# The first expert item of a fused attention and two expert layers: layer 1 in the attention's banks, half of its weights unsplit, two of its loads issued after the rows' gather

## The chip, the cores and the metric

One core of a Trainium2 chip runs the whole program. The metric is the device time of one execution in microseconds, the median of several runs. Every time below is in microseconds from the start of the program's span unless it is called a duration.

## The reference

Three layers in a row, all in f32: block-causal attention over 2 batches, 8 heads, 576 positions and 64 columns; an expert layer that sends each of the 1152 rows to the one of 8 experts with the largest logit; a second expert layer of the same size with a capacity of 288 rows per expert.

```python
scores = scale * np.matmul(q, k.transpose(0, 1, 3, 2))      # blocks of 64, masked above the diagonal
attn = np.exp(scores - np.max(scores, axis=-1, keepdims=True))
attn = attn / (np.sum(attn, axis=-1, keepdims=True) + 1e-09)
x = np.matmul(attn, v)                                      # then (1152, 512)

e_idx = np.argmax(x @ w_gate, axis=1)                       # per row one expert e
h = np.maximum(x[mask] @ w1[e], 0.0)                        # (rows, 512) x (512, 1024)
ye = h @ w2[e]                                              # (rows, 1024) x (1024, 512)
out[mask] = gate_w[mask, None] * eom[mask, e, None] * ye
```

The second layer has no output gate `eom` and leaves out the rows of an expert beyond its capacity.

## The kernel before

**Products.** TensorE multiplies f32 matrices exactly enough only in four passes, or as three one-pass products of `float32r` operands. The kernel splits each weight chunk (128 x 1024) into a high part, `wh = round(raw)`, which is a cast on ScalarE (`split_hi`, L147), and a low part, `wl = raw - wh`, a subtraction on VectorE (`split_lo`, L165). The rows are split the same way (`xh`, `xl` in `xprep`, L607 and L608; `hh`, `hl` between the layers). A product is then `xh*wh + xh*wl + xl*wh`: three products of 128 x 512 (L618 for layer 1, L632 for layer 2).

**Items.** An expert's rows are worked in items of 128 rows. Each item needs 8 chunks of weights, 4 of `w1` (512 x 1024) and 4 of `w2` (1024 x 512, two 128-row halves per chunk), in the tile `raw` (8 x 128 x 1024 f32, 512 KB a chunk), and its 128 rows, which an indirect DMA of POOL gathers from the attention's output in DRAM (`gather_rows`, L182). Layer 1 multiplies 4 row chunks by 4 weight chunks for each of two halves of 512 columns, relu on ScalarE (L677) brings a half to `hs`, four transposes (L713) turn it, `hh` and `hl` split it (L714, L716), and layer 2 adds 8 steps of three products into one bank. An item whose expert is that of the item before skips its loads.

**The order.** The attention part is put in order by a scheduler of the framework. From `tc.manual_schedule()` on, each engine runs its instructions in the order in which the code writes them. The first item (item 0) is prepared while the last head's attention runs: `begin_first` picks the expert of the first three blocks of rows (`route_first`), loads the four `w1` chunks once the expert is known (`first1["e"]`), gathers the rows once their numbers are known (`first1["ig"]`), and then loads the four `w2` chunks (`first1["e2"]` is the same expert's number, computed again after the rows' numbers, so that these loads are issued after the gather). Chunks 0 to 2 of `w1` are split beside the last attention products, and the cast of chunk 3 follows the last of the copies `ot` of the attention output (L1127 to L1129).

**Passing over.** The last steps of a head are: four f32 products with 64 columns of weights each (L1124), three copies to `ot` on ScalarE, two products with a matrix that sorts rows and adds the gate logits (L1138 and L1139), then on VectorE the scaling of the rows (L1142) and of the logits (L1144) and their sum (L1146). After it the attention's PSUM pools (`ps_s`, two tiles of two banks; `ps_t`, four banks) are closed and the expert layers' pool `ps_m` takes all eight banks (`PH` 2, `PX` 4, `PY` 1, `PR` 1). Only then does `xprep` transpose the gathered rows (L605).

**Route and first item.** `Moe.begin` weaves item 0 with the routing of all other rows: `step1` finds each row's expert (its last operation writes the one-hot `ohx`, L204), `step2` ranks rows on TensorE (L438, L440), `step3` is a chain of small VectorE operations (from `rko`, L448, to the last `ohp`, L497), `step4` gets every item's row numbers from 18 small products (L520) and writes them (`ig`, L522). Gathers of items 1 and 2 and the loads of item 1 follow. `go(n)` issues the first `n` products of layer 1; `parts(i)` transposes half `i`.

```python
some(split_hi, his, 2)
R.step1()
splits()
some(split_hi, his, 2)
go(n)
R.step2()
...
go(n1 // 2 + 3)
low0 = parts(0)
go(n1)
```

Here `his` are the casts of the four `w2` chunks, `splits` is `xl` and the low part of `w1` chunk 3. After layer 2 comes `xprep` of item 1 (L605, L607, L608), and item 1 goes on in `second` and `layers`.

Of the kernel before, what the change touches and what calls it, by code (L numbers as in the profile page):

```python
# [7 lines left out]
F32 = mybir.dt.float32  # L8
# [23 lines left out]
def kernel(  # L32
# [569 lines left out]
    def xprep(xg, ps, later=False):  # L602
# [5 lines left out]
        low = lambda: V.tensor_tensor(xl, ps, xh.bitcast(F32), op=ALU.subtract)  # L608
        if later:
            return (xh, xl), low  # L610
        low()
        return xh, xl

    def l1_steps(out_, xs, w, c, cols):
        xh, xl = xs
        wh, wl = w
        for j, (l, r) in enumerate(((xh, wh), (xh, wl), (xl, wh))):
            yield nc.tensor.matmul(out_, l[:, c * P : (c + 1) * P], r[:, cols], start=(c == 0 and j == 0), stop=(c == KD - 1 and j == 2))  # L618
# [5 lines left out]
    def l2_mm(y, ts, ws, f, start=None, stop=None):  # L624
        th, tl = ts[f // 4]
        wh, wl = ws[f // 2]
# [3 lines left out]
        rs = slice((f % 2) * 512, (f % 2 + 1) * 512)  # L630
        for j, (l, r) in enumerate(((th, wh), (tl, wh), (th, wl))):
            nc.tensor.matmul(y, l[:, cs], r[:, rs], start=(first and j == 0), stop=(last and j == 2))  # L632
# [11 lines left out]
    class Moe:  # L644
# [22 lines left out]
        def first_layer1(self, xs, ws):  # L667

            hs = HS.next()
            for i in range(2):  # L670
                ps = PH.next()
                n = 0
                for c in range(KD):
                    for _ in l1_steps(ps, xs, ws[c], c, slice(i * 512, (i + 1) * 512)):
                        n += 1
                        if n == 3 * KD:
# [3 lines left out]
        def begin(self, l1, n, gone, w2_done, splits):  # L680


            R, st = self.R, self.st
            n1 = 6 * KD
# [8 lines left out]
            his, los = iter(range(KD + w2_done, 2 * KD)), iter(range(KD + w2_done + (self.m == 2), 2 * KD))  # L693
# [15 lines left out]
            def parts(i):  # L709
                ps, th, tl = PX.next(), HH.next(), HL.next()  # L710
                h = self.h[:, i * 512 : (i + 1) * 512]
                for c in range(4):
                    nc.tensor.transpose(ps[:, c * P : (c + 1) * P], h[:, c * P : (c + 1) * P], ident)  # L713
                nc.scalar.copy(th, ps)  # L714
                ht.append((th, tl))
# [13 lines left out]
            for _ in range(2 if self.m == 1 else 0):  # L729
# [709 lines left out]
```

## Time and profile before

| | |
|---|---|
| median of three runs (lowest, highest) | 453.9 us (451.9, 454.22) |
| the profiled execution: its own time, its span | 451.8 us, 450.0 us |
| busy, share of the span: TensorE, VectorE, ScalarE, POOL | 92%, 82%, 73%, 22% |
| the chain that ended last: TensorE, VectorE, ScalarE, nothing seen | 70%, 15%, 6%, 6% |
| mean granted TensorE clock | 0.988 |
| q1 (loads and stores), q0 (gathers and scatters) | 54.62 MB, 10.63 MB |

The profile is of one execution, and all durations below are of that one. The span runs from the first to the last instruction; the execution's own time is 1.8 us more. Shares of busy time are means over stages with different limits: attention up to about 135 us, the first expert layer to about 307, then the second. A chain of waits goes back from the last instruction, at each step to whatever released it; the row of a step tells when it began and how long it ran on the chain. In the timeline the note in brackets is the time the engine stood idle before an instruction and what ended it. PE is TensorE, PEld its weight load, DVE VectorE, ACT ScalarE, SP the engine that issues the loads.

### The profile page before, as it was taken

The numbers are of one execution on the slowest core, as the hardware profiler recorded it, in microseconds if no ns is written. First come the engines' busy times: TensorE is split into PE (matmuls) and PEld (weight loads), VectorE is DVE, ScalarE is ACT, GpSimd is POOL, SyncE is SP. The second block draws the span as 40 slices with busy tenths as digits, with TensorE's granted clock in tenths as the row PEclk, the third lists the DMA queues.
The fourth block names the chain that finished last, engine by engine and source line by source line (L and its number), as shares of the span: only waits on it lengthen the run. The fifth ranks groups of instructions, "written<-read, shape, count | busy, mean of one in ns | idle before, by whom it ended". The sixth has DMA issues, their size and how long they took to land.

```text
span 450.0 us, 8362 instructions
## 1 busy us (share of the span) xinstructions
PE 414.7 (92%) x2501; PEld 334.0 (74%) x2501; DVE 368.4 (82%) x816; ACT 327.9 (73%) x617; POOL 99.0 (22%) x182
## 2 busy tenths in 40 slices
PE   3899999999988998999997999978989999999993
PEld 2677888877766776788876888755768888888872
DVE  8666776766799999989899796778899999999930
ACT  3678787787775889577868474645959988888930
POOL 8501221121020312033202203102303611111100
PEclk9999999999998999999999899999999999999998
DMA  5567532311074210199519102914628418995000
GB/s 133 110 175 243 133 79 53 82 28 52 20 280 153 72 47 18 32 320 338 194 47 360 63 13 83 348 49 133 259 95 311 146 52 305 395 375 206 24 31 8
DMA packets 58245, 65.99 MB, mean 147 GB/s; under 512 B 34080, under 2 KB 38688, under 8 KB 58180
## 3 DMA queue, kind: packets, MB, share of 16 engines
q1 hardware_dynamic: 54660, 54.62, 37.0%
q0 software_dynamic: 3520, 10.63, 6.8%
q8 instruction: 25, 0.41, 0.4%
q14 instruction: 40, 0.33, 0.2%
HBM read 109.66 MB, written 11.01 MB: 268 GB/s over the span
## 4 chain that ended last, share of the span: by engine, by line
PE 70%; DVE 15%; ACT 6%; issue 6%; DMA 1%; POOLq 0%; POOL 0%; DVEq 0%; ACTq 0%
PE ph L618 21%; PE py L632 20%; PE s L1071 7%; PE pst L1124 6%; PE pst L1098 5%; DVE wl L165 4%; PE px L1311 3%; PE px L605 2%; ACT p L1075 2%; DVE wl_a L165 2%; PE pst L1051 2%; PE px L1358 1%; DVE i128b L99 1%; DVE wl_b L165 1%; PE s L1068 1%
## 5 line engine op out<-in xcount | busy, mean ns | idle before, releaser
L165 DVE TENSOR_TENSOR wl<-raw,wh 128x1024 fp32r<-128x1024 f32 x84 | 98.8, 1217 | 2.6 <-ACT wh L147 2.5
L147 ACT CAST wh<-raw 128x1024 fp32r<-128x1024 f32 x84 | 82.7, 1058 | 1.0 <-DMA raw<-in_moe_w_dram 0.9
L618 PE MATMUL ph<-wh,xh 128*128 128x512 f32 x168 | 69.8, 416 | 2.5 <-ACT xh L607 2.1
L618 PE MATMUL ph<-wl,xh 128*128 128x512 f32 x168 | 67.0, 399 | 1.0 <-DVE wl L165 1.0
L618 PE MATMUL ph<-wh,xl 128*128 128x512 f32 x168 | 67.2, 400 | 0.1
L165 DVE TENSOR_TENSOR wl_a<-raw,wh_a 128x1024 fp32r<-128x1024 f32 x44 | 52.0, 1216 | 0.8 <-ACT wh_a L147 0.3
L147 ACT CAST wh_a<-raw 128x1024 fp32r<-128x1024 f32 x44 | 43.9, 1068 | 7.0 <-DMA raw<-in_moe_w_dram 7.0
L1072 DVE TENSOR_REDUCE mx<-s 128x1 f32<-128x256 f32 (+8 forms) x72 | 34.4, 486 | 17.7 <-PE s L1071 6.2
L165 DVE TENSOR_TENSOR wl_b<-raw,wh_b 128x1024 fp32r<-128x1024 f32 x40 | 47.4, 1219 | 0.9 <-ACT wh_b L147 0.5
L1075 ACT ACTIVATE p<-s,mx 128x256 f32<-128x256 f32 (+8 forms) x72 | 37.8, 527 | 10.0 <-DVE mx L1072 9.0
L147 ACT CAST wh_b<-raw 128x1024 fp32r<-128x1024 f32 x40 | 39.3, 1065 | 0.0
L1098 PE MATMUL pst<-ident,p 128*128 128x128 f32 x200 | 38.6, 286 | 0.4 <-DVE lg L1144 0.3
L618 PEld LDWEIGHTS ph<-wl,xh 128*128 128x128 f32 x168 | 32.1, 191 | 9.2 <-DVE wl L165 3.4
L618 PEld LDWEIGHTS ph<-wh,xh 128*128 128x128 f32 x168 | 31.9, 190 | 8.9 <-ACT xh L607 2.8
L618 PEld LDWEIGHTS ph<-wh,xl 128*128 128x128 f32 x168 | 31.9, 190 | 8.3 <-DVE xl L608 1.7
L632 PE MATMUL py<-wh_a,hh 128*128 128x512 f32 x88 | 35.9, 408 | 0.4 <-ACT hh L1319 0.4
L632 PE MATMUL py<-wh_a,hl 128*128 128x512 f32 x88 | 35.2, 400 | 0.8 <-DVE hl L716 0.5
L632 PE MATMUL py<-wl_a,hh 128*128 128x512 f32 x88 | 35.0, 398 | 0.0
L1302 ACT ACTIVATE hs<-ph 128x512 f32<-128x512 f32 x38 | 22.3, 602 | 16.9 <-PE ph L618 15.5
L641 POOL DMA_INDIRECT x2d<-ys,io x8 | 11.9, 1483 | 95.3 <-ACT ys L640 87.1
L1320 DVE TENSOR_TENSOR hl<-px,hh 128x512 fp32r<-128x512 f32 x38 | 24.4, 681 | 9.9 <-ACT hh L1319 9.9
L632 PE MATMUL py<-wh_b,hh 128*128 128x512 f32 x80 | 32.3, 404 | 0.0
(298 smaller groups left out, 901.5 us busy)
## 6 DMA issues: line engine op xcount, KB each, us to landing
raw<-in_moe_w_dram SPq DMA_DIRECT2D x184, 512.0 KB
out_dram<-zrow SPq DMA_DIRECT2D x9, 256.0 KB
kn<-in_k_dram SPq DMA_DIRECT2D x16, 128.0 KB
qn<-in_q_dram SPq DMA_DIRECT2D x16, 128.0 KB
vn<-in_v_dram SPq DMA_DIRECT2D x16, 128.0 KB
x1d<-x SPq DMA_DIRECT2D x3, 576.0 KB
x2d<-zrow SPq DMA_DIRECT2D x3, 256.0 KB
x1d<-x SPq DMA_DIRECT2D x3, 192.0 KB
```

What stands on the lines that cost most here:

```text
L147: nc.scalar.copy(whs[i], raw[:, c, :])
L165: V.tensor_tensor(wls[i], raw[:, c, :], whs[i].bitcast(F32), op=ALU.subtract)
L618: yield nc.tensor.matmul(out_, l[:, c * P : (c + 1) * P], r[:, cols], start=(c == 0 and j == 0), stop=(c == KD - 1 and j == 2))
L632: nc.tensor.matmul(y, l[:, cs], r[:, rs], start=(first and j == 0), stop=(last and j == 2))
L1071: nc.tensor.matmul(ps[:, a:z], s[l][:, b, :], s[r][:, a - o : z - o], start=(j == 0), stop=(j == 2))
L1072: V.tensor_reduce(out=s["mx"][:, t : t + 1], in_=ps[:, o : o + n], op=ALU.max, axis=AX.X, negate=True)
L1075: nc.scalar.activation(s["p"][b][:, 0:n], ps[:, o : o + n], AF.Exp, bias=s["mx"][:, t : t + 1], accum_out=s["sm"][:, t : t + 1])
L1098: last[0] = nc.tensor.transpose(ps[:, j * P : (j + 1) * P], s["p"][b][:, c * P : (c + 1) * P], ident).ins
L1124: nc.tensor.matmul(po[r, 0 : n * BLK], nat["v"][h % NR["v"]][:, c, r], w[:, :, r], start=(c == 0), stop=(c == nc_ - 1))
L1302: nc.scalar.activation(hs[:, i * 512 : (i + 1) * 512], hp[i], AF.Relu)
L1311: nc.tensor.transpose(ps[:, c * P : (c + 1) * P], hs[:, o : o + P], ident)
L1320: V.tensor_tensor(tl, tps[i], th.bitcast(F32), op=ALU.subtract)
```

## The change

For item 0 of the first layer alone:

- **Banks.** The attention pools stay open longer (`banks`, closed by `open_banks` inside `begin`, after the routing's `step3` is issued). The gathered rows are transposed into an attention bank `pst`, on TensorE's queue ahead of the last four attention products, and layer 1's two halves go to a tile `hp0` of `ps_s`.
- **Whole chunks.** Chunks 2 and 3 of `w1` and chunks 0 and 1 of `w2` are not split: one f32 product of `raw` with unsplit rows stands for three. The rows are first copied unsplit, `xn` (in `YS.t[1]`), and only their first 256 columns are split, from `xn`; `hn` is the unsplit first half of the turned `hs`. The whole products come first in each half.
- **Loads.** Chunks 0 and 1 of `w1` are loaded as before; chunks 2 and 3 are loaded after the gather, ahead of the `w2` chunks.
- **Order in `begin`.** The two casts that are left for `w2` are issued after `parts(0)`, the second half's transposes come after `step3`, one of layer 2's steps ahead of `step4` and three behind it.
- **Last head.** The logits are scaled before the rows (L1144 and L1142 change places for the last head).

```diff
-    def l1_steps(out_, xs, w, c, cols):
-        xh, xl = xs
-        wh, wl = w
-        for j, (l, r) in enumerate(((xh, wh), (xh, wl), (xl, wh))):
-            yield nc.tensor.matmul(out_, l[:, c * P : (c + 1) * P], r[:, cols], ...)
+    def l1_steps(out_, xs, w, c, cols, start=None, stop=None):
...
+        if w is None:
+            yield nc.tensor.matmul(out_, xs[2][:, cs], raw[:, c, cols], start=start, stop=stop)
+            return
+        for j, (l, r) in enumerate(((xs[0], w[0]), (xs[0], w[1]), (xs[1], w[0]))):
+            yield nc.tensor.matmul(out_, l[:, cs], r[:, cols], start=start and j == 0, stop=stop and j == 2)
...
     def l2_mm(y, ts, ws, f, start=None, stop=None):
...
+        if ws[f // 2] is None:
+            nc.tensor.matmul(y, th[:, cs], raw[:, KD + f // 2, rs], start=first, stop=last)
+            return
...
+            order = sorted(range(KD), key=lambda c: ws[c] is not None)
+            self.half = sum(3 if w else 1 for w in ws)
...
-            some(split_hi, his, 2)
+            if m == 2:
+                some(split_hi, his, 2)
             R.step1()
             splits()
-            some(split_hi, his, 2)
+            if m == 2:
+                some(split_hi, his, 2)
             go(n)
             R.step2()
...
+                if ws2[2 * i] is None:
+                    ht.append((HN, None))
+                    nc.scalar.copy(HN, ps)
+                    return lambda: None
...
-            go(n1 // 2 + 3)
+            go(self.half + 3)
             low0 = parts(0)
-            go(n1)
+            if m == 1:
+                some(split_hi, his, 2)
+            go(2 * self.half)
             chain, regs, places = R.step3(), R.registers(), R.places_a()
...
+            if m == 1:
+                open_banks()
+                low1 = parts(1)
+                self.y = PY.next()
+                l2(0, 1)
             some(split_lo, los, 1)
             low0()
             R.step4()
...
             some(split_lo, los, 4)
+            if m == 1:
+                l2(1, 4)
...
-                    load_w(w11, w12, first1["e"], 0, KD)
+                    load_w(w11, w12, first1["e"], 0, 2)
                 yield
             xg = item0["xg"] = XG.next()
             g = gather_rows(xg, x1d[0 : NA * P, :], first1["ig"]).ins
-            load_w(w11, w12, first1["e2"], KD, 8)
+            load_w(w11, w12, first1["e2"], 2, 8)
...
-        for c, (w, h, pk) in ((1, ("ot", H - 1, 1)), (2, ("tp", H - 1, 2)), (3, ("ot", H - 1, 2))):
-            with tc.issue_after(anchors[w, h, pk]):
-                item0["w1"].append(split(c) if c < KD - 1 else split_hi(c))
+        with tc.issue_after(anchors["ot", H - 1, 1]):
+            item0["w1"] += [split(1), None, None]
         ctx.enter_context(tc.manual_schedule())
+
+        ps, xn, xh, xl = pst(), YS.t[1], XH.next(), XL.next()
+        for c in range(KD):
+            nc.tensor.transpose(ps[:, c * P : (c + 1) * P], item0["xg"][:, c * P : (c + 1) * P], ident)
+        z = 2 * P
+        with tc.issue_after(anchors["ot", H - 1, 2]):
+            nc.scalar.copy(xn, ps)
+            nc.scalar.copy(xh[:, 0:z], xn[:, 0:z])
...
-    one.begin(one.first_layer1(item0["xs"], item0["w1"]), 2, 0, 0, first_splits)
+    hp0 = ps_s.tile([P, 1024], F32, tag="s", name="hp0")
+    one.begin(one.first_layer1(item0["xs"], item0["w1"], [hp0[:, 0:512], hp0[:, 512:1024]]), 4, 0, 0, 2, first_low)
```

Three places show how the instructions move. The first is TensorE at the end of the last head: `tp` and `vn` are the turned attention weights and the values, `xg` the gathered rows, `ph` (before) and `hp` (now) layer 1's banks, `ys` the copy `xn`. Before:

```order
L1124 MATMUL pst<-tp_2_1_2010,vn_193 64x192 x2
L1124 MATMUL pst<-tp_2_1_2010,vn_193 64x64 x2
L1124 MATMUL pst<-tp_2_2_2017,vn_193 64x64 x4
L1138 MATMUL pst<-mv_235,ot_238 128x160
L1139 MATMUL pst<-mv_235,ot_238 128x80
L605 MATMUL px_2148<-ident,xg_148 128x128 x4
L618 MATMUL ph_2146<-wh_140,xh_153 128x512
L618 MATMUL ph_2146<-wl_144,xh_153 128x512
```

and now:

```order
L1151 MATMUL pst<-tp_2_1_2008,vn_193 64x192 x2
L1151 MATMUL pst<-tp_2_1_2008,vn_193 64x64 x2
L1295 MATMUL pst<-ident,xg_148 128x128 x4
L1151 MATMUL pst<-tp_2_2_2015,vn_193 64x64 x4
L1165 MATMUL pst<-mv_235,ot_238 128x160
L1166 MATMUL pst<-mv_235,ot_238 128x80
L617 MATMUL hp_2146<-raw,ys_152 128x512 x2
L620 MATMUL hp_2146<-wh_140,xh_153 128x512
L620 MATMUL hp_2146<-wl_144,xh_153 128x512
```

The transposes of `xg` went from behind L1139 to a place ahead of the last four attention products, and two whole products open layer 1.

The second is ScalarE from the routing's exponential (`ex`) to the end of item 0; `wh_a` are the high parts of the `w2` chunks, `hh` those of the turned half. Before (the casts of the first two `w2` chunks stand ahead of it):

```order
L206 ACTIVATE ex_2170<-d_2163 128x72
L147 CAST wh_a_2129<-raw 128x1024
L147 CAST wh_a_2130<-raw 128x1024
L677 ACTIVATE hs_2135<-ph_2146 128x512
L714 CAST hh_2136<-px_2150 128x512
L677 ACTIVATE hs_2135<-ph_2147 128x512
L218 ACTIVATE so_2297<-so_2297 128x9
L714 CAST hh_2137<-px_2148 128x512
```

and now:

```order
L206 ACTIVATE ex_2156<-d_2149 128x72
L685 ACTIVATE hs_2134<-hp_2146 128x512
L732 COPY hn<-pst 128x512
L147 CAST wh_a_2128<-raw 128x1024
L147 CAST wh_a_2129<-raw 128x1024
L685 ACTIVATE hs_2134<-hp_2146 128x512
L736 CAST hh_2135<-px_2255 128x512
L218 ACTIVATE so_2294<-so_2294 128x9
```

The two casts that are left went from ahead of the first half's relu to a place between `hn` and the second half's relu.

The third is TensorE at the start of layer 2: `ohp`, `ra` and `rb` belong to the routing's placing products (18 of them, the last or first shown), `py` is layer 2's bank. Before:

```order
L520 LDWEIGHTS ohp_2246
L520 MATMUL px_2151<-rb_2249,ohp_2246 128x17
L713 MATMUL px_2148<-ident,hs_2135 128x128 x4
L632 MATMUL py_2152<-wh_a_2127,hh_2136 128x512
L632 MATMUL py_2152<-wh_a_2127,hl_2138 128x512
L632 MATMUL py_2152<-wl_a_2131,hh_2136 128x512
L632 MATMUL py_2152<-wh_a_2127,hh_2136 128x512
```

and now:

```order
L620 MATMUL hp_2146<-wl_145,xh_153 128x512
L620 MATMUL hp_2146<-wh_141,xl_155 128x512
L729 MATMUL px_2255<-ident,hs_2134 128x128 x4
L633 MATMUL py_2259<-raw,hn 128x512
L520 LDWEIGHTS ohp_2225
L520 MATMUL px_2256<-ra_2227,ohp_2225 128x17
```

The placing products went from ahead of the second half's transposes to a place behind the first step of layer 2. On SP's queue the order is now chunks 0 and 1, the store of the second row block of `x1d`, chunks 2 and 3 and the four `w2` chunks; before, chunks 2 and 3 stood with 0 and 1.

## Rows read from the trace of the kernel before

**Rows 1.** The chain of waits, 118 to 153: start us, us, what

```profile
118.17 0.27 PE pst L1138 x2
...
136.08 0.64 PE px L605 x4
137.43 0.73 PE ph L618 x2
...
145.88 0.61 ACT hs L677
...
146.53 0.66 PE px L713 x4
147.18 5.49 PE py L632 x24
152.67 0.45 PE px L605 x4
```

**Rows 2.** The timeline, 132 to 138: start us, us, engine, operation, [idle before, releaser]

```profile
133.65 1.22 DVE L165 TENSOR_TENSOR wl<-raw,wh 128x1024 fp32r<-128x1024 f32 x1
133.72 0.27 ACT L1127 COPY ot<-pst 128x128 f32<-128x128 f32 x1
134.37 0.54 PE L1138 MATMUL pst<-mv,ot 128*128 128x160 f32 x2 [0.75 <-ACT ot L1129]
134.75 0.34 PE L1139 MATMUL pst<-mv,ot 128*128 128x80 f32 x2
135.78 0.20 DVE L1144 TENSOR_TENSOR lg<-pst,ri 128x48 f32<-128x48 f32 x1
136.08 0.63 PE L605 MATMUL px<-ident,xg 128*128 128x128 f32 x4 [0.99 <-DVE lg L1144]
137.39 0.23 DVE L204 TENSOR_TENSOR ohx<-im,first 128x72 bf16<-128x72 f32 x1
```

**Rows 3.** Stretches: us, busy us of each engine (instructions), granted clock, DMA share, GB/s

```profile
135.09:138.49 3.40, 1.69 (x18) 1.21 (x18) 2.98 (x12) 2.00 (x4) 0.00 (x0) 1.00 1.00 365
138.49:141.90 3.41, 3.41 (x9) 2.64 (x9) 3.38 (x19) 2.98 (x4) 0.00 (x0) 0.50 0.38 131
153.80:187.00 33.20, 29.93 (x160) 22.84 (x161) 32.99 (x55) 26.52 (x34) 7.47 (x7) 1.00 0.13 40
```

**Rows 4.** The timeline again, 139 to 154, VectorE's routing and TensorE's placing products

```profile
139.27 0.23 DVE L448 TENSOR_TENSOR rko<-px,a_kx 128x72 f32<-128x72 f32 x1
...
143.44 0.90 DVE L497 TENSOR_SCALAR ohp<-i128b,pp 128x128 bf16<-128x128 bf16 x5
145.68 0.39 PE L520 MATMUL px<-ra,ohp 128*128 128x17 bf16 x9
145.93 0.37 PE L520 MATMUL px<-rb,ohp 128*128 128x17 bf16 x9
...
153.76 0.69 DVE L608 TENSOR_TENSOR xl<-px,xh 128x512 fp32r<-128x512 f32 x1 [0.58 <-ACT xh L607]
```

**Rows 5.** The timeline: the gather on POOL, loads on SP, casts on ScalarE

```profile
129.74 1.16 POOL L182 DMA_INDIRECT xg<-x1d,a_ids  x1 [7.46 <-DVE a_gs L340]
130.99 2.87 SPq L177 DMA_DIRECT2D raw<-in_moe_w_dram  x4
137.27 2.00 ACT L147 CAST wh_a<-raw 128x1024 fp32r<-128x1024 f32 x2
140.92 1.04 ACT L147 CAST wh_a<-raw 128x1024 fp32r<-128x1024 f32 x1 [0.21 <-DMA raw<-in_moe_w_dram]
```

**Rows 6.** DMA issues, 146 to 150: operation xcount, median us from issue to landing

```profile
xg<-x1d,ig POOLq DMA_INDIRECT x2, 3.5
```

**Rows 7.** DMA queues, 132 to 133: packets, MB, share of 16 engines

```profile
q1 hardware_dynamic: 234, 0.18, 55.2%
q0 software_dynamic: 62, 0.21, 51.3%
```

**Rows 8.** DMA queues, 133 to 135

```profile
q0 software_dynamic: 18, 0.05, 8.2%
```

More of the change, by code (lines that the diff above doesn't have):

```diff
@@ L665, in load, with first_layer1, begin @@
             load_w(self.w1, self.w2, e, c0, c1, cond=cond)
-        def first_layer1(self, xs, ws):
+        def first_layer1(self, xs, ws, banks=None):
             hs = HS.next()
+            order = sorted(range(KD), key=lambda c: ws[c] is not None)
+            self.half = sum(3 if w else 1 for w in ws)
             for i in range(2):
-                ps = PH.next()
+                ps = banks[i] if banks else PH.next()
                 n = 0
-                for c in range(KD):
-                    for _ in l1_steps(ps, xs, ws[c], c, slice(i * 512, (i + 1) * 512)):
+                for c in order:
+                    for _ in l1_steps(ps, xs, ws[c], c, slice(i * 512, (i + 1) * 512), c == order[0], c == order[-1]):
                         n += 1
-                        if n == 3 * KD:
+                        if n == self.half:
                             nc.scalar.activation(hs[:, i * 512 : (i + 1) * 512], ps, AF.Relu)
                         yield hs
-        def begin(self, l1, n, gone, w2_done, splits):
-            R, st = self.R, self.st
-            n1 = 6 * KD
+        def begin(self, l1, n, gone, w2_done, whole, splits):
+            R, st, m = self.R, self.st, self.m
             def go(upto):
@@ L691, in go @@
                     gone += 1
-            his, los = iter(range(KD + w2_done, 2 * KD)), iter(range(KD + w2_done + (self.m == 2), 2 * KD))
+            k0 = KD + w2_done + whole
+            his, los = iter(range(k0, 2 * KD)), iter(range(k0 + (m == 2), 2 * KD))
+            ws2 = [None if w2_done <= c < w2_done + whole else (whs[KD + c], wls[KD + c]) for c in range(KD)]
             def some(f, cs, k):
@@ L728, in begin @@
             R.step4()
-            for _ in range(2 if self.m == 1 else 0):
+            for _ in range(2 if m == 1 else 0):
                 next(places)
@@ L741, in begin @@
             some(split_lo, los, 4)
+            if m == 1:
+                l2(1, 4)
+            else:
+                self.y = PY.next()
             self.load(1, KD)
[L745 to L751 removed]
+            l2(4 if m == 1 else 0, 6)
             ws = st["w1"][1] = [split_hi(c) for c in range(KD)]
@@ L935, with pst @@
     route2 = Route(2, lg2[:, :, 0:E], None, capf, first2)
+    banks = ctx.enter_context(ExitStack())
+    ps_s = banks.enter_context(tc.tile_pool(name="ps_s", bufs=2, space=PSUM))
+    ps_t = banks.enter_context(tc.tile_pool(name="ps_t", bufs=4, space=PSUM))
+    def pst():
+        return ps_t.tile([P, 512], F32, tag="t", name="pst")
     with ExitStack() as actx:
@@ L1282, with open_banks @@
     NR_ = ring(mp1, [P, NT, E + 1], F32, "nr", 2)
-    PH = ring(ps_m, [P, 512], F32, "ph", 2)
-    PX = ring(ps_m, [P, 512], F32, "px", 4)
-    PY = ring(ps_m, [P, 512], F32, "py", 1)
-    PR = ring(ps_m, [P, 512], F32, "pr", 1)
-    rings = [XG, XH, XL, HS, HH, HL, YS, YT, NQ, NR_, PH, PX, PY]
+    HN = mp1.tile([P, 512], F32, name="hn")
+    PH = PX = PY = PR = rings = None
+    def open_banks():
+        nonlocal PH, PX, PY, PR, rings
+        banks.close()
+        ps_m = ctx.enter_context(tc.tile_pool(name="ps_m", bufs=1, space=PSUM))
+        PH = ring(ps_m, [P, 512], F32, "ph", 2)
+        PX = ring(ps_m, [P, 512], F32, "px", 4)
+        PY = ring(ps_m, [P, 512], F32, "py", 1)
+        PR = ring(ps_m, [P, 512], F32, "pr", 1)
+        rings = [XG, XH, XL, HS, HH, HL, YS, YT, NQ, NR_, PH, PX, PY]
+        route1.pst = route2.pst = PX.next
     def layer1(xs, ws, after=()):
```

56 lines of the change are left out of this document (27 added, 29 removed).

## The prediction

> **What bounds the kernel now.** I read the chain of waits first, for 118 to 155 us, because the change touches only the passage from the last attention head to the second item of the first expert layer. The chain there is a relay [rows 1]: the four transposes of the gathered rows (136.08), the first layer-1 product (137.43), the relu of the second half (145.88), its transposes (146.53), layer 2 (147.18 to 152.67), the transposes for item 1. Then the timeline says what stood ahead of each [rows 2]. The last attention products end at 135.09 (134.75 + 0.34), yet the row transposes start only at 136.08: the new PSUM pool gets its banks when VectorE has read the last attention bank (logit scaling, 135.78), and VectorE was late because it had split weight chunk 2 from 133.65 for 1.22 us. Third, the stretches [rows 3]: TensorE was busy for 1.69 of the 3.40 us from 135.09 to 138.49, and for the next 3.41 us its granted clock was 0.50, the 1.2 GHz level of the two (the other, 2.4, is 1.00). Fourth, what follows: from 153.8 to 187 VectorE is busy 32.99 of 33.20 us [rows 3], and what starts that stretch is `xl` of item 1 at 153.76, before which VectorE had stood 0.58 us for the rows that follow layer 2 [rows 4]. So a shift of the end of layer 2 is passed on almost whole, while VectorE work saved ahead of that point is only worth what layer 2 gains by it.
>
> **The change, part by part.** I work against the profiled execution (451.8 us, span 450.0). The median of the three runs is 453.9, so 2.1 us are added at the end.
>
> *The start of layer 1.* The row transposes now stand on TensorE's queue ahead of the last four attention products, in an attention bank, so no bank has to be handed over. Behind them wait those four products, the three `ot` copies on ScalarE, L1138/L1139 and all of VectorE's routing. What they wait for is the gather. It was issued at 129.74 [rows 5]. Lower bound for its landing: a gather on idle queues took 3.5 us [rows 6], so 133.2. Upper bound: here 62 of its 80 packets moved between 132 and 133 [rows 7] and 18 between 133 and 135 [rows 8], so about 135.2. The two loads that used to run ahead are now issued from about 131.0, where the first layer-2 load was issued (130.99 [rows 5]), so the load queue is empty when the gather starts, but not while it runs. I take 133.7, nearer the idle row. Four transposes take 0.45 (152.67 in [rows 1]); the last products and their drain I put at as much, an estimate; from the first `ot` copy to the end of L1139 it is 1.37 (133.72 to 135.09 [rows 2]). The new copy `xn` follows the third `ot` copy (L1138 waits for that one and began at 134.37, so 0.6 in) and takes some 0.6 like the relu, so it is hidden beside L1138/L1139. First product: 133.7 + 0.45 + 0.45 + 1.4 = 136.0, against 137.43: **1.4 us earlier**. The routing one-hot is needed two whole products and two short ones later, at 138.2; it ends 2.5 us after L1139 instead of 135.09 to 137.62 (the VectorE split is gone and the logits go first, so I take 2.1), at 138.1. No wait there.
>
> *The products.* Whole f32: two passes of 160 columns took 0.27 us [rows 1], so 512 columns take 0.86. The three split ones it replaces took 3 x 5.49/24 = 0.69 [rows 1]. Layer 1 had 24 split products, one transpose group and the small routing products in 145.85 - 137.43 = 8.42 us. Of that 24 x 0.229 = 5.49, transposes 0.66, routing some 0.25; 1.7 is half of the 3.41 us at half clock, 0.3 small waits. Now 4 whole and 12 split are 6.2, with 0.9 for the same rest 7.1: layer 1 ends at 143.1, 2.7 us earlier than 145.85.
>
> *Between the layers.* Before, the relu came 0.03 after the last product, and layer 2 started 1.3 us after it. Now ScalarE's queue holds, ahead of the second relu, the copy `hn` and the two casts of layer-2 chunks 2 and 3. `hn` can start when the first half's transposes are through, five short products before layer 1 ends, at 141.95, and ends at 142.55; two casts took 2.00 [rows 5], so 144.55. The relu 0.61 and the transposes 0.66 put the first layer-2 product at 145.85. TensorE stands idle from 143.1 to 145.2. **This takes back 1.4 us.** Are the chunks there? Before, chunk 3 of layer 2 landed at 140.92 [rows 5]. Six loads and the gather, 3.4 MB, at the 365 GB/s of [rows 3] from 132 on are 9.3 us: 141.3, and it is wanted at 143.55. Spare, but not much.
>
> *Layer 2.* Four whole and 12 split products: 3.46 + 2.75. The 18 placing products (145.68 to 146.30 [rows 4]) stood beside the relu before; now they stand inside layer 2 and cost their 0.6. Together 6.8 against 5.49: **1.3 us more**. VectorE's routing chain took 139.27 to 144.34 [rows 4]; from 138.6 it ends at 143.7, three us before it is asked. Its last `hl` needs the two remaining splits and comes at about 149.8, when the four whole products end (149.9). The end: 145.85 + 6.8 = 152.65, against 152.67.
>
> *What VectorE and ScalarE no longer do.* Four 1.22 us splits, half of one x split and one `hl` (0.69 is what such a half-width operation takes [rows 4]), 5.9 us of VectorE, and four casts less two small copies on ScalarE. Nothing of it counts further: `xl` of item 1 still waits for layer 2. The two loads moved behind the gather count through the landing times above; SP issues the same number, in the order chunks 0 and 1, x store, chunks 2 and 3, layer 2.
>
> *The clock.* At the full clock the sum is zero. Before, the half clock followed a stretch in which TensorE stood in pieces while it waited for copies and for its banks. Those pieces shrink, but the new wait of 2.1 us between the layers stands in one piece, and in it TensorE has nothing at all to do. I think it more likely than not that the clock falls there too. The same 3.41 us at 1.2 GHz cost 1.7, of which 0.2 falls on waits that layer 2 has anyway: **+1.5 us**.
>
> The sum: -1.4 (start), -1.3 (layer 1 in itself, the old half clock gone), +1.4 (wait for two casts), +1.3 (layer 2), +1.5 (new half clock) = +1.5: 453.3 for the profiled execution, **455.4 us** beside the median. The same sum without the last term is 453.9.
>
> Two rules speak against parts of this. First the row: 62 of the gather's 80 packets moved within 1 us while the load queue was taking 55% of the engines [rows 7], so it did not queue behind the loads. The Trainium skill (DMA: Bandwidth & Descriptors, Queues, rings and completion order) says that each engine takes turns between the queues it has work for; by that rule a load moved behind the gather frees little, and the gather would land as late as before, at 135.2. By the rows the tail of 18 packets did lag, so the rule covers most of it and not all.
>
> And on the clock: by the rows it fell after several short waits, none over 1 us [rows 2]. The Trainium skill (TensorE: Matmul & The Clock Gate, HAM oscillation) puts such a fall down to one long wait for a transfer; by that, neither the old waits nor the new one would be charged, and the time would be 453.9. The old fall speaks against it.
>
> **The rivals.**
>
> *No fall of the clock.* The wait between the layers is a single one, and TensorE is busy before and after it. Then the earlier start and the dearer products cancel: 453.9; with the gather at 133.2, 453.4.
>
> *Slower: the gather holds the end of attention.* Until now only the expert layer waited for the gather; now the last four attention products, and with them `ot`, the logits and the routing, stand behind it on TensorE's queue. At 135.2 instead of 133.7 everything above moves by 1.5 us: 455.4 + 1.5 = 456.9. It decides from a landing of about 134.5 on, together with the fall of the clock. For it: the six loads are issued just as it starts, and its tail lagged before. Against: the queue ahead of it is empty, and most packets moved in 1 us even when it was not. That the move behind the gather doesn't free the gather is the same rival.
>
> *Faster: VectorE is the true bound.* It is busy nearly without a break from 136 to 187, and loses 5.9 us. If layer 2 were not what starts `xl`, VectorE alone could be there earlier: from the end of its routing chain at 143.7 it has four splits (4.9), one `hl` (0.7) and some 0.9 of small steps left, 150.2 instead of 153.76, 3.6 us earlier: 450.3. For it: 32.99 of 33.20 us [rows 3]. Against: the 0.58 us that it stood before `xl`, and the two casts ahead of the relu, which no VectorE work removes.
>
> **How the numbers follow.** Half a per cent is 2.3 us, about what a measurement of this kernel can tell from no change; the three runs lie 2.3 us apart. Forecast with the half clock 0.42, no fall 0.30, late gather 0.17, VectorE 0.11. The first two lie within half a per cent, but 0.07 of the forecast's spread goes over 456.2 (a gather at 134.5 does it) and 0.02 of the second under 451.6. That gives 0.13 faster, 0.63 same, 0.24 slower. The range goes up to the late gather's 456.9, so half of that case lies above it, and down to 452.2, which leaves out the VectorE case: not quite 0.2 in all.
>
> **What would show it.** Row transposes starting between 133.3 and 134.5, with the last attention products behind them; the first whole product near 136.0, and pairs of them 1.7 us apart; a gap on TensorE of 2 us before the relu of the second half, ended by ScalarE, with two casts in it; a granted clock of 0.5 just after it; layer 2 of 6.8 us or more; VectorE standing over 1 us ahead of `xl` of item 1. I am wrong if that gap is under 1 us, if the transposes start after 135, or if `xl` of item 1 comes before 152.

## The result, and the profile after the change

The changed kernel took 458.2 us, the median of three runs (455.86 to 459.76), against 453.9 before; the ratio is 1.0101, with a 95% interval of 1.0057 to 1.0145. A second series, of 8 runs against 25, gave 1.008 (1.0042 to 1.0118). Ratios leave out runs in the slower of two states that some executions show: 1 of these 25, and 2 of 23 further below. So it is slower by 3.6 to 4.6 us: above the range I gave, and on the other side of the half per cent from most of my chance. The profiled execution took 458.2 us, its span is 456.5.

The chain of waits of the changed kernel, 148 to 157 us (start us, us, what), answers to [rows 1]. Row transposes of item 1 are L605 in both, the whole layer-2 products are L633, the split ones L637:

```profile
148.10 0.51 ACT hs L685
...
148.66 0.66 PE px L729 x4
149.31 0.86 PE py L633 x2
150.17 0.44 PE px L520 x18
150.62 2.67 PE py L633 x6
153.29 2.77 PE py L637 x12
156.07 0.45 PE px L605 x4
```

Item 1 starts at 156.07 instead of 152.67, 3.4 us later. The two profiled executions differ by 6.5 us of span; the other 3.1 us come behind item 0, where two executions of the kernel before differ by 2.3 as well (e7). What led to the 3.4 us shows in the timeline. TensorE first, which answers to [rows 2]:

```profile
134.39 0.63 PE L1295 MATMUL pst<-ident,xg 128*128 128x128 f32 x4 [1.21 <-DMA xg<-x1d,a_ids]
134.95 0.45 PE L1151 MATMUL pst<-tp,vn 128*64 128x64 f32 x8
136.16 0.54 PE L1165 MATMUL pst<-mv,ot 128*128 128x160 f32 x2 [0.75 <-ACT ot L1156]
136.77 3.50 PE L617 MATMUL hp<-raw,ys 128*128 128x512 f32 x4
...
142.94 1.99 PE L617 MATMUL hp<-raw,ys 128*128 128x512 f32 x4 [0.74 <-ACT hs L685]
...
148.66 0.66 PE L729 MATMUL px<-ident,hs 128*128 128x128 f32 x4 [1.90 <-ACT hs L685]
```

Three waits stand here. The row transposes wait for the gather until 134.39, and the last attention products wait behind them. The whole products of the second half wait 0.74 us for the relu of the *first* half, which nothing in the arithmetic asks for: both halves are written into one tile, `hp0`, and writing its right half is held until the relu has read its left one. And 1.90 us go before the second half's transposes. What ScalarE did in that time:

```profile
142.29 0.60 ACT L685 ACTIVATE hs<-hp 128x512 f32<-128x512 f32 x1 [3.90 <-PE hp L620]
145.63 0.59 ACT L732 COPY hn<-pst 128x512 f32<-128x512 f32 x1 [2.74 <-PE pst L729]
146.11 1.99 ACT L147 CAST wh_a<-raw 128x1024 fp32r<-128x1024 f32 x2
148.00 0.60 ACT L685 ACTIVATE hs<-hp 128x512 f32<-128x512 f32 x1
```

The last product of layer 1 ended near 146.7; the relu stands behind two casts until 148.00. The gather, in the list of DMA issues (operation, count, us from issue to landing), took 4.7 us from its issue at 129.54, so it landed at 134.2, against the 3.5 us of [rows 6]:

```profile
xg<-x1d,a_ids POOLq DMA_INDIRECT x1, 4.7
```

Two stretches (us, busy us of PE, PEld, DVE, ACT, POOL, granted clock, DMA share, GB/s), answering to [rows 3]:

```profile
133.70:137.10 3.40, 1.95 (x17) 1.60 (x18) 0.28 (x3) 1.51 (x5) 0.00 (x0) 1.00 0.98 358
137.10:140.51 3.41, 3.41 (x6) 1.33 (x4) 1.95 (x9) 0.32 (x2) 0.00 (x0) 0.50 1.05 398
```

The half clock has not gone: it falls on the first whole products. VectorE, which before had stood 0.58 us ahead of `xl` of item 1 [rows 4], now stands longer and starts later:

```profile
157.16 0.69 DVE L608 TENSOR_TENSOR xl<-px,xh 128x512 fp32r<-128x512 f32 x1 [1.85 <-ACT xh L607]
```

To compare executions I read six times out of every timeline: the gather's issue, the starts of the row transposes, of the first product, of the two relus, and of item 1's row transposes. The issue of the gather itself comes at 128.0 to 128.1 in some executions and at 129.5 to 129.8 in others, of either kernel, so times are counted from there. The column on the half clock says how many of these us were at it; the last column takes half of them off, which is what they cost at most, and shows the difference from the 21.1 of the kernel before too.

| kernel, execution | gather to transposes | to first product | to first relu | to second relu | to item 1 | sum | half clock | at full clock |
|---|---|---|---|---|---|---|---|---|
| before, first | 6.34 | 1.35 | 5.03 | 3.42 | 6.63 | 22.8 | 3.4 | 21.1 |
| before, again | 6.64 | 1.34 | 4.82 | 3.43 | 6.62 | 22.9 | 3.4 | 21.2 |
| changed, first | 4.85 | 2.38 | 5.52 | 5.71 | 7.91 | 26.4 | 3.4 | 24.7 (+3.6) |
| changed, again | 4.63 | 2.37 | 3.82 | 5.72 | 7.90 | 24.4 | 0 | 24.4 (+3.3) |
| two tiles | 5.40 | 2.37 | 3.82 | 4.72 | 7.90 | 24.2 | 0 | 24.2 (+3.1) |
| transposes last | 5.42 | 1.27 | 3.87 | 5.72 | 7.87 | 24.2 | 0 | 24.2 (+3.1) |
| casts late | 4.52 | 2.38 | 3.82 | 4.50 | 7.89 | 23.1 | 0 | 23.1 (+2.0) |
| loads first | 5.55 | 1.30 | 3.82 | 5.72 | 9.38 | 25.8 | 3.4 | 24.1 (+3.0) |
| three waits out | 5.23 | 1.27 | 4.16 | 3.50 | 7.90 | 22.1 | 0 | 22.1 (+1.0) |
| banks alone | 6.74 | 1.31 | 4.97 | 3.41 | 7.29 | 23.7 | 3.4 | 22.0 (+0.9) |
| layer 2 split | 5.25 | 1.27 | 7.21 | 2.90 | 9.33 | 26.0 | 6.8 | 22.6 (+1.5) |
| banks and loads | 7.27 | 1.28 | 6.32 | 3.42 | 7.25 | 25.5 | 6.8 | 22.1 (+1.0) |

### The profile page after: what moved, and what is told of

Same layout as the page of the kernel before. It is cut to its first block, busy times and chain, and to the rows that moved or that the text cites. A ratio compares the mean times of both kernels' runs of the same rounds, so it can differ in the third digit from the quotient of the medians.

```text
span 456.5 us, 8344 instructions
## 1 busy us (share of the span) xinstructions
PE 421.7 (92%) x2493; PEld 335.8 (74%) x2493; DVE 363.4 (80%) x811; ACT 324.6 (71%) x614; POOL 96.9 (21%) x182
## 4 chain that ended last, share of the span: by engine, by line
PE 49%; DVE 10%; issue 3%; ACT 3%; DMA 1%; POOLq 0%; DVEq 0%; ACTq 0%
PE py L637 21%; PE ph L620 20%; PE px L1358 3%; DVE wl L165 2%; DVE wl_a L165 2%; PE px L1405 2%; PE px L605 2%; DMA raw<-in_moe_w_dram 1%; DVE wl_b L165 1%; DVE hl L1367 1%; PE py L633 1%; ACT wh L147 1%; ACT xh L607 1%; PE px L1387 1%; DVE xl L608 1%
## 5 line engine op out<-in xcount | busy, mean ns | idle before, releaser
L165 DVE TENSOR_TENSOR wl<-raw,wh 128x1024 fp32r<-128x1024 f32 x82 | 96.4, 1221 | 2.5 <-ACT wh L147 2.5
L147 ACT CAST wh<-raw 128x1024 fp32r<-128x1024 f32 x82 | 80.6, 1058 | 2.0 <-DMA raw<-in_moe_w_dram 2.0
L620 PE MATMUL ph<-wh,xh 128*128 128x512 f32 x160 | 66.7, 417 | 1.7 <-ACT xh L607 1.3
L620 PE MATMUL ph<-wl,xh 128*128 128x512 f32 x160 | 64.6, 404 | 1.0 <-DVE wl L165 1.0
L620 PE MATMUL ph<-wh,xl 128*128 128x512 f32 x160 | 64.6, 404 | 0.1
L165 DVE TENSOR_TENSOR wl_a<-raw,wh_a 128x1024 fp32r<-128x1024 f32 x42 | 49.8, 1222 | 1.7 <-ACT wh_a L147 1.2
L147 ACT CAST wh_a<-raw 128x1024 fp32r<-128x1024 f32 x42 | 41.8, 1067 | 6.5 <-DMA raw<-in_moe_w_dram 6.5
L620 PEld LDWEIGHTS ph<-wl,xh 128*128 128x128 f32 x160 | 30.7, 192 | 9.1 <-DVE wl L165 3.5
L620 PEld LDWEIGHTS ph<-wh,xl 128*128 128x128 f32 x160 | 30.7, 192 | 7.9 <-DVE xl L608 1.7
L637 PE MATMUL py<-wh_a,hh 128*128 128x512 f32 x84 | 35.4, 421 | 0.4 <-ACT hh L1366 0.4
L637 PE MATMUL py<-wh_a,hl 128*128 128x512 f32 x84 | 34.1, 405 | 0.8 <-DVE hl L737 0.5
L637 PE MATMUL py<-wl_a,hh 128*128 128x512 f32 x84 | 33.8, 403 | 0.0
L637 PE MATMUL py<-wh_b,hh 128*128 128x512 f32 x80 | 32.8, 410 | 0.0
## 6 DMA issues: line engine op xcount, KB each, us to landing
kn<-in_k_dram SPq DMA_DIRECT2D x16, 128.0 KB
qn<-in_q_dram SPq DMA_DIRECT2D x16, 128.0 KB
vn<-in_v_dram SPq DMA_DIRECT2D x16, 128.0 KB
```

The source lines that it names most:

```text
L147: nc.scalar.copy(whs[i], raw[:, c, :])
L165: V.tensor_tensor(wls[i], raw[:, c, :], whs[i].bitcast(F32), op=ALU.subtract)
L620: yield nc.tensor.matmul(out_, l[:, cs], r[:, cols], start=start and j == 0, stop=stop and j == 2)
```

## The experiments

The first four each take one suspect out of the changed kernel; they ran together, beside 8 runs of the kernel before (median 452.36).

**Two tiles (e1).** Each half of layer 1 gets a PSUM tile of its own.

```diff
+    hp1 = ps_s.tile([P, 1024], F32, tag="s", name="hp1")
-    one.begin(one.first_layer1(item0["xs"], item0["w1"], [hp0[:, 0:512], hp0[:, 512:1024]]), 4, 0, 0, 2, first_low)
+    one.begin(one.first_layer1(item0["xs"], item0["w1"], [hp0[:, 0:512], hp1[:, 0:512]]), 4, 0, 0, 2, first_low)
```

> Layer 1's two halves get a bank tile each, in place of the two halves of one tile. Theory of the waits: the second half's first whole product stood 0.74 us for the first half's relu (142.94 in the changed kernel) only because both halves are one tile; it now follows the first half at once, and the transposes of item 1, at 155.91 in the changed kernel and 152.51 before, start near 155.2. Rival, the dearer products: what costs is eight whole products and the placing products inside layer 2, some 2 us that no wait explains; the 0.74 us gap closes but the two casts ahead of the second relu take it back, and item 1's transposes stay at 155.7 to 155.9.

Ratio 1.0123 (1.0088 to 1.0158), median 457.51. The time does not show it, the trace does: the wait of the second half's products is gone,

```profile
140.79 0.39 PE L620 MATMUL hp<-wh,xl 128*128 128x512 f32 x1
141.02 1.88 PE L617 MATMUL hp<-raw,ys 128*128 128x512 f32 x4
```

and from relu to relu it is 4.72 us instead of 5.72. So the one tile costs 1.0 us. The gather happened to take 0.8 us longer than in the changed kernel's second execution, which hid most of it in the sum.

**Transposes last (e2).** The row transposes go behind L1166, where attention ends, and keep their attention bank.

```diff
+        with tc.issue_after(last[0]):
             for c in range(KD):
                 nc.tensor.transpose(ps[:, c * P : (c + 1) * P], item0["xg"][:, c * P : (c + 1) * P], ident)
```

> The transposes of the gathered rows go behind L1139 on TensorE's queue, instead of ahead of the last four attention products. Theory of the waits: the last attention products no longer stand 1.21 us for the gather (transposes at 134.39 in the changed kernel); L1138 starts near 134.0 instead of 136.16, the routing's one-hot is ready near 136.8 instead of 138.9, the first whole product starts near 136.0 instead of 136.77, and item 1's transposes start near 155.1 (from 155.91). Rival: the first whole product needs the copy of the turned rows anyway, so the start moves by 0.3 us at most and the end with it, 155.6 or later.

Ratio 1.0136 (1.0092 to 1.0179), median 457.18. Attention's end comes 5.58 us after the gather's issue, not 7.1 or 7.3 us, and the first product 6.69 us after it, where the changed kernel has 7.00 and 7.23. So ahead of the last attention products the transposes gain nothing, since both wait in one queue: 0.3 to 0.5 us are lost by it in these executions. The time does not show it.

**Casts late (e3).** The two casts of layer-2 chunks 2 and 3 go behind the second relu.

```diff
-            if m == 1:
-                some(split_hi, his, 2)
             go(2 * self.half)
+            if m == 1:
+                some(split_hi, his, 2)
```

> The two casts of layer-2 chunks go behind the second half's relu on ScalarE. Theory of the waits: the relu follows the last layer-1 product at once (in the changed kernel the product ended near 146.6 and the relu began at 148.00), layer 2 starts 1.4 us earlier, and item 1's transposes start near 154.5. Rival: the casts are wanted by layer 2 right after, so what is won there is waited for in the split steps of layer 2; item 1's transposes no earlier than 155.5.

Ratio 1.0065 (1.0002 to 1.0128), median 455.74, the best of the four. ScalarE of this kernel:

```profile
142.10 0.59 ACT L732 COPY hn<-pst 128x512 f32<-128x512 f32 x1 [2.75 <-PE pst L729]
143.26 0.60 ACT L685 ACTIVATE hs<-hp 128x512 f32<-128x512 f32 x1 [0.57 <-PE hp L620]
143.75 1.98 ACT L147 CAST wh_a<-raw 128x1024 fp32r<-128x1024 f32 x2
```

The relu now waits for the product, and from relu to relu it is 4.50 instead of 5.72; the rest keeps its 7.9 us, so later casts cost nothing. The order of the two casts is worth 1.2 us.

**Loads first (e4).** All four first loads are issued ahead of the gather again, as before the change; this also moved the row transposes behind L1151's products, one place later on TensorE.

```diff
-                    load_w(w11, w12, first1["e"], 0, 2)
+                    load_w(w11, w12, first1["e"], 0, KD)
-            load_w(w11, w12, first1["e2"], 2, 8)
+            load_w(w11, w12, first1["e2"], KD, 8)
```

> All four layer-1 chunks are loaded ahead of the gather, as before the change; all else as changed. If the move of two loads frees the gather, the row transposes (134.39 in the changed kernel) now start near 135.4 and item 1's transposes near 156.8, about 1 us later. Rival: the gather shares the queues in either order, and the row transposes start within 0.3 us of 134.4; item 1's transposes at 155.6 to 156.2.

Ratio 1.0115 (1.0069 to 1.016), median 456.36. The transposes start 5.55 us after the gather's issue, named by the gather; with the loads behind it, it was 4.52 to 5.40 where the gather is named, so this one execution does not settle it (more under e6). In this execution the clock fell where my forecast had put the fall, just after the wait for the two casts:

```profile
142.80:146.20 3.40, 1.50 (x8) 0.79 (x7) 1.23 (x1) 2.61 (x4) 0.00 (x0) 1.00 0.00 0
146.20:149.60 3.40, 3.40 (x22) 1.68 (x21) 2.23 (x6) 1.81 (x4) 1.51 (x2) 0.50 0.03 12
```

The next four ran together, beside 25 runs of the kernel before (median 453.83).

**Three waits out (e5).** e1, e2 and e3 in one kernel.

> The changed kernel with its three new waits taken out together: the two halves of layer 1 in two tiles, the row transposes behind the last four attention products, the two casts of layer-2 weights behind the second half's relu. Measure used: from the issue of the first gather to item 1's row transposes (before 22.8 us with a clock fall inside, after 26.4 us with one). Waits theory (item 0's loss is those waits plus dearer products): first product 6.7 us after the gather's issue, then about 15.3 us, so 22.0 us without a clock fall and 23.7 with one; if item 0 is all of the loss, the ratio to before is 0.995 to 1.003. Rival, dear products (whole float32 products and the placing products cost it): 24 us or more also without the waits, ratio 1.006 or more. Rival, the loss lies behind item 0: 22.0 us here, yet a ratio of 1.006 or more, with the blocks of layer 2 falling behind one after another later.

Median 454.12, ratio 1.002 (0.9985 to 1.0056): no longer to be told from the kernel before. From the gather's issue to item 1's transposes it is 22.06 us, 22.0 expected. The single gains add up: from the changed kernel's 24.4, the sum 1.0 + 1.2 + 0.3 leaves 21.9. What is left at the full clock is 1.0 us more than before: the start gains 1.2, from the first product to the second relu 0.9 more is spent, and from there to item 1 another 1.3. The dearer products stand in both, and the placing products in the second; no run splits the two.

**The banks alone (e6).** The kernel before, with item 0's layer 1 in the attention's banks, all split, the loads where they were.

```diff
+        ps, xh, xl = pst(), XH.next(), XL.next()
+        with tc.issue_after(last[0]):
+            for c in range(KD):
+                nc.tensor.transpose(ps[:, c * P : (c + 1) * P], item0["xg"][:, c * P : (c + 1) * P], ident)
...
+            if self.m == 1:
+                open_banks()
```

> The kernel before with one part of the change alone: item 0's layer 1 runs in the attention's banks, its row transposes right behind the last attention product; no weight stays whole, the loads stand ahead of the gather as before. Waits theory: the 0.99 us wait of the row transposes for the logits' scaling goes; transposes 5.4 us and first product 6.7 us after the gather's issue, gather to item 1's transposes 21.8 us with a clock fall and 20.1 without; ratio 0.994 to 1.000. Rival, dear products: the same, as no product changes form here. Rival, VectorE the true bound of the start: item 1's transposes move by under 0.4 us, ratio 0.998 to 1.002. Rival, the banks kept open longer are themselves the loss behind item 0: ratio over 1.004.

Median 454.4, ratio 1.0022 (0.9998 to 1.0046): no gain in time. TensorE of this kernel:

```profile
134.89 0.34 PE L1143 MATMUL pst<-mv,ot 128*128 128x80 f32 x2
136.57 0.63 PE L1269 MATMUL pst<-ident,xg 128*128 128x128 f32 x4 [1.34 <-DMA xg<-x1d,a_ids]
...
146.91 0.38 PE L520 MATMUL px<-ra,ohp 128*128 128x17 bf16 x9 [0.69 <-ACT hs L677]
```

With no bank to wait for, the transposes wait for the gather, 6.74 us after its issue. That does not make the gather the cause in the kernel before, for it was later here. The DMA queues show it (packets, MB, share; q0 is the gathers' queue). The kernel before, 134.70 to 134.85, then 134.85 to 136.10:

```profile
q0 software_dynamic: 1, 0.00, 0.4%
...
q1 hardware_dynamic: 236, 0.46, 100.5%
```

This kernel, 135.70 to 136.00, then 136.00 to 136.60:

```profile
q0 software_dynamic: 1, 0.00, 0.2%
...
q1 hardware_dynamic: 126, 0.24, 104.4%
```

So the gather's last packet moved 5.1 us after the issue in the kernel before and 6.2 us after it here. Where the gather is named as the releaser (e1, e3, e4, e6, both executions of the changed kernel), the transposes start 0.4 to 0.6 us after its last packet. In the kernel before it is 1.2 us: by this estimate the gather would have let them start 0.6 to 0.8 us earlier there, and this much was the bank's handover, as the row says. In e7, the same kernel once more, it is 0.64 us, and the two ended together. Which of them comes last changes from one execution to the next.

The second surprise is the third line of TensorE: the new banks are opened once the second relu has read the old ones, so the 18 placing products, which stood beside the relu before, now stand behind it; from the second relu to item 1 it is 7.29 instead of 6.63. The handover had not gone, it had moved.

**The kernel before, again (e7)**, unchanged.

> The kernel before, unchanged, to see how one execution differs from the next. If the later part of the loss (about 3 us behind item 0) is luck of the execution: the blocks of layer 2 behind item 0 shift by 2 us or more against the first profile of the same kernel, and the clock falls at other places. If it belongs to the change: every block within 1 us of the first profile (after the shift of its start is taken off), the clock falling near 138 and 247 us again.

One execution, 452.45 us. Item 0 repeats to 0.1 us. Behind it this execution lost 2.3 us against the first profile of the same kernel (at the last layer-2 block, with the shift of item 0 taken off), with four falls of the clock where that had one. In the changed kernel's two executions the same difference is 3.1 and 2.0 us.

**The changed kernel, again (e8)**, unchanged.

> The changed kernel, unchanged. Gather to item 1's transposes: 26.4 us if the clock falls among the first products again, 24.6 us if it doesn't (both theories of item 0). If the later loss belongs to the change, it again loses about 3 us behind item 0, with falls near 250, 291 and 304 us; if it is luck, the later shift lies between 0 and 4 us and the falls lie elsewhere. Ratio 1.006 to 1.014 as before.

Median 456.93, ratio 1.008 (1.0042 to 1.0118). 24.44 us, as expected without a fall among the first products, and the later falls lie elsewhere (181, 297 and 338 us). The first three falls of the first execution after item 0 had been at 185, 250 and 291.

The last two ran beside 23 runs of the kernel before (median 453.8).

**Layer 2 split (e9).** e5 with all of layer 2 split, its casts at the places that they have in the kernel before.

```diff
-    one.begin(one.first_layer1(item0["xs"], item0["w1"], [hp0[:, 0:512], hp1[:, 0:512]]), 4, 0, 0, 2, first_low)
+    one.begin(one.first_layer1(item0["xs"], item0["w1"], [hp0[:, 0:512], hp1[:, 0:512]]), 4, 0, 0, 0, first_low)
...
-            if m == 2:
-                some(split_hi, his, 2)
+            some(split_hi, his, 2)
```

> The changed kernel with the three waits out (two tiles, row transposes last, no casts ahead of the second relu), and layer 2 of item 0 all split again as in the kernel before, its casts back at the places they had there; layer 1 keeps its two whole chunks, two of the loads stay behind the gather. Theory (layer 2's dearer products and the placing products inside it cost 1.2 us; VectorE has room for the two further splits): from the gather's issue to item 1's row transposes 20.9 us with no clock fall (22.1 with layer 2 half whole), ratio to before 0.996 to 1.000. Rival, VectorE or ScalarE is then late for layer 2 (two more casts of 1.0 and two more splits of 1.2 us): 21.9 us or more, ratio 1.000 to 1.004.

Median 455.97, ratio 1.0046 (1.0017 to 1.0075), so no better than e5: the rival held, and more of it than it had priced. ScalarE, and TensorE at the last line:

```profile
138.67 2.18 ACT L147 CAST wh_a<-raw 128x1024 fp32r<-128x1024 f32 x2 [2.10 <-DMA raw<-in_moe_w_dram]
...
142.44 1.04 ACT L147 CAST wh_a<-raw 128x1024 fp32r<-128x1024 f32 x1 [0.24 <-DMA raw<-in_moe_w_dram]
143.39 0.59 ACT L685 ACTIVATE hs<-hp 128x512 f32<-128x512 f32 x1
144.13 0.63 PE L727 MATMUL pst<-ident,hs 128*128 128x128 f32 x4 [2.26 <-ACT hs L685]
```

With two loads behind the gather all of layer 2's loads come later too, and the first relu stands behind casts that wait for them: from the first product to the first relu 7.21 us instead of 4.16. Chunks left whole in layer 2 cost 1.3 us from the second relu on (7.90 instead of 6.63), but with late loads, splitting them all was no cheaper.

**Banks and loads (e10).** e6, with two of the four first loads behind the gather.

> The kernel before with layer 1 in the attention's banks, all split, and two of the four first loads behind the gather. Theory (the row transposes waited as much for the gather as for the banks; loads behind it bring its landing 1.2 us forward): transposes 5.4 us after the gather's issue instead of 6.7 with the banks alone, first product 6.7 us; gather to item 1's transposes 22.2 us with a clock fall (23.7 with the banks alone), ratio 0.996 to 1.001. Rival, the loads that were moved come too late for the last two chunks' splits: the products of chunks 2 and 3 wait for them, 23 us or more, ratio 1.001 to 1.006. Rival, the gather lands no earlier: transposes 6.3 us or more after its issue, ratio 1.002 as with the banks alone.

Median 455.26, ratio 1.006 (1.003 to 1.0089). The gather landed 4.3 us after its issue, so the move does bring it forward, but the transposes started only 7.27 us after it:

```profile
133.26 1.04 ACT L147 CAST wh<-raw 128x1024 fp32r<-128x1024 f32 x1 [2.28 <-DMA raw<-in_moe_w_dram]
134.21 0.26 ACT L1131 COPY ot<-pst 128x128 f32<-128x128 f32 x1
134.85 0.54 PE L1142 MATMUL pst<-mv,ot 128*128 128x160 f32 x2 [2.93 <-ACT ot L1133]
```

The cast of chunk 2 stands ahead of attention's last copies on ScalarE, and its load is now late: attention itself ends later. The rival had named the load, but put the wait at the products of chunks 2 and 3.

**Whether the rest is the clock's.** Each timed run has its mean granted clock beside it. The time at half clock in a run is twice the missing share: for the 24 runs before that enter the ratio, mean clock 0.9797, 2 x 0.0203 x 453.3 = 18.4 us; for the changed kernel's 8 runs beside them, 0.9799, it is 18.4 too. So the two kernels spend the same time at the half clock, and the 3.5 us between the means of these runs (456.8 and 453.3) are not the clock's. Taking half of it off every run, and setting that beside what the timelines show of item 0:

| kernel | runs: mean us at full clock, against before (95%) | item 0 at full clock, against before |
|---|---|---|
| changed, again | +3.5 (1.1) | +3.3 to +3.6 |
| two tiles | +3.0 (2.8) | +3.1 |
| transposes last | +3.6 (2.3) | +3.1 |
| casts late | +2.6 (1.7) | +2.0 |
| loads first | +4.1 (2.4) | +3.0 |
| three waits out | +1.6 (1.0) | +1.0 |
| banks alone | -0.4 (1.7) | +0.9 |
| layer 2 split | +1.3 (1.0) | +1.5 |
| banks and loads | +1.0 (0.9) | +1.0 |

Every pair agrees within the interval: the change of item 0's passage is all of the loss that these runs can see. The 3.1 us lost behind item 0 in the first profile of the changed kernel are no sign against it: the kernel before loses 2.3 us there in its own second profile.

## Why the prediction was wrong

My sum, ordered by cause, was: start -1.4; layer 1 +0.4 (its -1.3 without the 1.7 of the old half clock); wait for the casts +1.4; layer 2 +1.3; and the clock -1.7 + 1.5. That is +1.7 of work and -0.2 of clock. Measured in work: +3.3 to +3.6.

- **The start was mis-sized: -0.7, not -1.4.** From the gather's issue to the first product it is 7.0 and 7.2 us, against 7.7 and 8.0 before. I took 4.0 us for the gather's landing, near the idle row [rows 6]; in the profile after it took 4.7, in e9 and e10 4.6 and 4.3, and where a row names it the transposes started 4.5 to 5.4 after its issue. From the transposes to the first product I had 2.3, and it is 2.4. I had argued that the load queue would be empty; but six loads are issued right behind the gather, two at 130.46 and four from 131.66, and it runs beside them. The late gather, which I had as a rival at 5.5 us, was half true. What I drew from the rule against the change (the Trainium skill, DMA: Bandwidth & Descriptors, Queues, rings and completion order), a landing as late as before, is not what the traces show either: with the loads ahead the gather's last packet moved 5.0 to 6.2 us after its issue (four executions, mean 5.5), with two of them behind it 4.0 to 5.0 (eight, mean 4.3), so moving them brings it forward by some 1.2 us.
- **The old wait was one execution's.** I gave the 0.99 us of [rows 2] to VectorE's logits, and to the banks, because the row names them. For that execution this is right, though only 0.6 to 0.8 us of it would have gone with the banks; in e7 the gather ended with them, and e6, with no bank to hand over, starts no earlier. The gain that repeats comes from the loads.
- **The wait within layer 1 was not foreseen: +1.0.** I costed the products of both halves as one run of 7.1 us. That the two halves are slices of one tile stands in the diff, and e1 shows its price.
- **The wait for two casts was right.** A gap of 2.1 us on TensorE was expected, 1.90 is there with two casts in it, and e3 gets 1.2 of the 1.4 us back by moving them.
- **Layer 2 was right.** +1.3 expected; from the second relu to item 1 it is 7.90 against 6.63, +1.3.
- **The clock was right in amount and wrong as an argument.** I had the old half clock go and a new one come after the wait for the casts. In the changed kernel's first profile it came among the first whole products, in the second not at all in item 0; after the wait for the casts it came in e4 and not in the four other executions that have this wait. The old fall did mostly go: it came among the first products in all four executions with layer 1 all split (before, e6, e7, e10), and in one of the eight with whole chunks there. But over whole runs the two kernels do not differ in the time at the half clock, so -1.7 was no gain to book: falls avoided here turned up elsewhere. That the two clock terms together came near the truth was luck.
- **The faster rival is out.** VectorE stands 1.85 us ahead of `xl` of item 1, and its start moved with layer 2.

Start and one tile make the difference: 0.7 + 1.0 = 1.7, between the +1.7 forecast and some +3.4 found. Of the signs that I had listed, most came (transposes at 134.39, the gap with two casts in it, layer 2 of 6.8 us, VectorE standing ahead of `xl`; not the first product near 136.0, which came at 136.77, nor the fall of the clock behind the gap): they tested the terms that I had, and none asked for a term that was missing.

## What to carry to other kernels

Two slices of one tile were one object to whatever orders the work here: before costing a run of products as gapless, ask of each output tile who still reads any part of it. A wait's releaser is only the last of several, and which one is last can change from one execution to the next: before you price its removal, find when the others ended, in more than one execution. And book no gain for a fall of the clock that a shorter wait avoids, unless whole runs show less time at the lower clock.

## What was not expected of the hardware

The granted clock did not follow from how long TensorE had been busy, or had waited, just before. Ahead of the first products the changed kernel's two executions look much the same, with waits of 1.21 and 0.75 us in the first and of 0.73 and 0.75 in the second, and yet the first fell to 0.50 (the rows at the top) and the second, here, did not:

```profile
131.62:135.02 3.40, 1.92 (x24) 1.44 (x18) 0.72 (x6) 1.18 (x5) 0.28 (x1) 1.00 0.87 324
135.02:138.42 3.40, 3.40 (x22) 2.00 (x20) 2.69 (x13) 0.65 (x2) 0.00 (x0) 1.00 1.03 393
```

TensorE was busy for 1.92 of 3.40 us here, for 1.95 there. In e1 it had waited longer (1.62 us for the gather) and was busy for less, and the clock stayed up too:

```profile
134.04:137.44 3.40, 1.62 (x16) 1.30 (x16) 0.00 (x0) 1.18 (x5) 0.00 (x0) 1.00 0.83 272
137.44:140.84 3.40, 3.40 (x22) 2.05 (x21) 2.69 (x13) 0.65 (x2) 0.00 (x0) 1.00 1.05 405
```

The wait for the casts gives the same picture: in e4 1.50 busy of the 3.40 us ahead, and a fall; in the changed kernel's second execution 1.49, and none:

```profile
143.20:146.60 3.40, 1.49 (x9) 0.82 (x9) 1.23 (x1) 2.54 (x4) 0.00 (x0) 1.00 0.00 0
```

The Trainium skill (TensorE: Matmul & The Clock Gate, HAM oscillation) ties such falls to one long wait for a transfer. e9 comes nearest to it, where TensorE stood 2.26 us behind casts that waited for loads and the clock was then at 0.50 for 6.8 us; the first fall of the changed kernel does not, since the waits ahead of it were 1.21 and 0.75 us. What decides between two executions that look alike stays open here.
